# Two-layer expert kernel after windowed attention: routing in groups of 4, 2, 2, 2, 2 and visits of two tiles at the end

## The chip, the core and the metric

The kernel runs on one core of one Trainium2 chip. The metric is device time in microseconds (us) of one execution; the number given is the median of three. Beside it stands one execution taken with the hardware profiler, from which all rows below come.

## What is computed

```python
def reference(q, k, v, n_global, n_local, ...):
    # 2 batches, 8 heads, 768 tokens, head size 64; 8 global keys, a window of 96
    attn_out = _attn_ref(q, k, v, n_global, n_local)      # softmax over the window and the global keys, ALiBi bias
    x = attn_out.transpose(0, 2, 1, 3).reshape(1536, 512)
    x = _moe_ref(x, ...)          # RMS norm; (silu(xn @ w_gate) * (xn @ w_val)) @ w_out, d_ff 1536
    return _moe2_ref(x, ...)      # noisy top-2 routing over 8 experts, then relu(x @ w1[e]) @ w2[e], d_ff 1024

def _moe2_ref(x, w_gate, w_noise, noise, w1, w2):
    noisy_logits = x @ w_gate + np.log1p(np.exp(x @ w_noise)) * noise
    top2 = np.argpartition(-noisy_logits, 2, axis=1)[:, :2]
    top2_w = softmax of the two chosen logits
    for e in range(8):
        for k in range(2):
            mask = top2[:, k] == e
            h = np.maximum(x[mask] @ w1[e], 0.0)
            out[mask] += top2_w[mask, k, None] * (h @ w2[e])
```

The weights of the first layer and the inputs are 64-bit floats that the kernel converts word by word (`conv`). Products are made in a split form: each operand is a rounded high part (h) and a remainder (l), and TensorE multiplies h by h, h by l and l by h.

## The kernel before

The 1536 tokens are 12 tiles of 128. Three stages run one after the other and overlap at their borders.

**Attention.** 12 tiles of 4 units (pairs of heads) each. `scores`, `turn` and `values` of a unit are spread over three slots; `norm` transposes the finished tile into `xTh`/`xTl`. The first 12 slots run alone, the others are worked in between the steps of the first layer (`side`). In the same time `feed` calls `conv`, which converts one block of the first layer's weights: ScalarE takes the absolute value (L517), VectorE clips, shifts and merges words (L518 to L525; the clip goes to GpSimd for blocks f of 2 and more), and a block of `g`, `v` and `o` is three conversions. Blocks with f of 2 and more are ordered behind tile 1's norm (`after`), those with f of 0 and 1 are not.

**First layer.** The 12 blocks of d_ff lie in four chunks (`CHUNKS`: 0 to 2, 3 to 5, 6 and 7, 8 to 11). `VISITS` is the list of (chunk, first tile, number of tiles). A step is one f of one visit: `up` makes 12 matmuls for the gate and 12 for the value (L572), `hidden` makes the tanh (L580), two VectorE products (L581, L582), the split dh (L585) and dl (L586), and `finish`, one step later, calls `down` (L599). A step of two tiles has both products in one bank of PSUM (`pz`, 256 columns each), one of four tiles in two (`pg`, `pv`, 512 columns each). Attention's scratch memory (pool `at`) is closed when attention is written out, and pool `late`, called "b" in the code, takes its place; `hidden` takes its u, dh and dl from "b" once that is there. After the last chunk a tile is complete: it is stored to `x2d` in HBM on SyncE's queue (L612), and when the tiles of a routing group are complete, `route` is called.

**Routing.** `GS` is the list of group sizes in tiles. For a group, `route` transposes its tiles (L649), computes the router's logits (L653), two activations (L661, L662), the top 2, the prefix sums that give each token its slot (L680 to L683), and writes token number and weight to the table `metad` by one indirect DMA of GpSimd for each tile and choice (L729, "scatters"): two for each tile. After group `LEAD` the expert with the most tokens so far is chosen (`lead`), and SyncE reads its number (L916).

**Second layer.** `units[0]` and `units[1]` both work that expert: unit 0 its first 256 slots, from the groups up to `LEAD`, and unit 1 the other 256. Seven more units, one for each other expert, follow in the order that the last group's counts give (`order`, L745, read by SyncE at L967). A unit fetches its slots (`me`, L768), clips them (`ic`, L777), gathers the rows of `x2d` with indirect DMAs (`xg`, L786), transposes them (`pg`, L796; L798, L799) and runs `up` (L822) and `down` (L844 or L838) on weights that SyncE loads (`wab`, L752 and L755) and ScalarE, VectorE and GpSimd split (`sa`, `sb`: L556, L558). Unit 1's slots are fetched after group `LEAD + 1`; the last group, which comes later than that fetch, is added to them on the chip (`late_slots`: `idf` L624, `hot` L629, matmuls L634, then `ic`). Each unit adds its result to `out` by a gather (L804) and a scatter (L876).

A scheduler at build time sets the order of instructions on each engine from the program text and its own estimate of durations; so an edit in one place can move instructions elsewhere. Each engine runs its own list in order and waits at an instruction whose inputs are not there; a DMA that SyncE, ScalarE or GpSimd issues is such an instruction of its list. Buffers of one tag rotate: a new tile waits until the last reader of the old one is done.

Of the kernel before, what the change touches and what calls it, by code (L numbers as in the profile page):

```python
# [9 lines left out]
F32 = mybir.dt.float32  # L10
# [9 lines left out]
P = 128  # L20
# [85 lines left out]
def fused(ctx: ExitStack, tc: tile.TileContext, q, k, v, n_global, n_local, w_gate, w_val, w_out,  # L106
# [12 lines left out]
    FB2 = F2 // P  # L119
    GS = [4, 4, 2, 2]  # L120
    NG = len(GS)
    G0 = [sum(GS[:g]) for g in range(NG)]
    LEAD = 1
    ST = 4
    CHUNKS = [[0, 1, 2], [3, 4, 5], [6, 7], [8, 9, 10, 11]]
    VISITS = [(0, 2 * i, 2) for i in range(6)] + [(1, 4 * i, 4) for i in range(3)]
    VISITS += [(c, t, 4) for c in (2, 3) for t in (0, 4)] + [(2, 8, 4), (3, 8, 2), (3, 10, 2)]
    FEED = [0, 0, 1, 0, 2, 2, 2, 2, 2, 3, 3]
    START = 12
    LAG = 8  # L130
    NRAW = {"a": 12, "b": 8}
    NACC = 8
# [375 lines left out]
    def conv(nm, f, src):  # L508
# [11 lines left out]
        sh = nc.vector.tensor_scalar(wi, wi, 3, 0x3FFFFFF8, op0=ALU.logical_shift_left, op1=ALU.bitwise_and)  # L520
        if late:
            after(ab, "A", 1)
            after(sh, "V", 1)
        nc.vector.scalar_tensor_tensor(wi, hi, -0x40000000, wi, op0=ALU.bitwise_and, op1=ALU.bitwise_or)
# [50 lines left out]
    def hidden(ci, f, t0, nt, pg, pv):  # L575
        GN = nt * P
        hp = pools.get("b", at)
        wd = 512 if "b" in pools else 256
        u = hp.tile([P, wd], F32, name=f"u{t0}_{f}", tag="u", bufs=1)[:, :GN]
        nc.scalar.activation(u, pg, AF.Tanh, scale=0.5)  # L580
        nc.vector.scalar_tensor_tensor(u, u, 1.0, pg, op0=ALU.add, op1=ALU.mult)  # L581
        nc.vector.scalar_tensor_tensor(u, u, 0.5, pv, op0=ALU.mult, op1=ALU.mult)  # L582
        dh = hp.tile([P, wd], F32R, name=f"dh{t0}_{f}", tag="dh", bufs=2)
        dl = hp.tile([P, wd], F32R, name=f"dl{t0}_{f}", tag="dl", bufs=2)
        nc.scalar.activation(dh[:, :GN], u, AF.Copy)  # L585
        (nc.gpsimd if ci < len(CHUNKS) - 1 else nc.vector).tensor_sub(dl[:, :GN], u, dh[:, :GN].bitcast(F32))  # L586
        return dh, dl

    def down(ci, t0, nt, f, d):
# [12 lines left out]
        for t in range(nt):  # L602
# [7 lines left out]
            if ci == len(CHUNKS) - 1:  # L610
                x2t[ti] = accs[ti]
                nc.sync.dma_start(x2d[ti * P:(ti + 1) * P, :], accs[ti])  # L612
        if t0 + nt == NT // P:
# [26 lines left out]
    def route(g):  # L640
# [3 lines left out]
        for t in range(GT):  # L644
            ti = G0[g] + t
            pt = ps.tile([P, 512], F32, name=f"pr{ti}", tag="ts"[t % 2 if last else 0])
            p3 = pt.rearrange("p (a b) -> p a b", a=DC)
# [241 lines left out]
    while n < START:  # L889
        slot(n, 0)  # L890
        slot(n, 1)
        if n in (3, 6, 9):
            feed(3)
        n += 1
    prev = None
    todo = []
# [13 lines left out]
    def finish(ci, t0, nt, f, d):  # L910
        down(ci, t0, nt, f, d)
        if ci == len(CHUNKS) - 1 and f == CHUNKS[ci][-1] and t0 != G0[-1]:
            g = G0.index(t0)
            route(g)
            if g == LEAD:
                r = nc.sync.value_load(lead.bitcast(I32)[:1, :1], min_val=0, max_val=E - 1)  # L916
                units[0].e = units[1].e = r
            if g == LEAD + 1:
                units[1].fetch()

    for vi, (ci, t0, nt) in enumerate(VISITS):
# [9 lines left out]
        for f in CHUNKS[ci]:  # L931
# [19 lines left out]
            prev = (ci, t0, nt, f, d)  # L951
            if (ci, t0) == (2, 8):
                if f == CHUNKS[ci][1]:
                    units[0].slots()
                    units[0].gather(0)
                    units[0].gather(1)
            if ci == 3 and t0 >= 8:
                k = CHUNKS[ci].index(f) + (4 if t0 == 10 else 0)
                if k in (2, 3):
                    units[0].turn(k - 2)  # L960
                moe2_weights(0, units[0].e, k)
    finish(*prev)
# [116 lines left out]
```

## Time and profile before

| what | value |
| --- | --- |
| three executions | 867.02, 864.85, 859.6 us; median 864.85 |
| profiled execution | 865.25 us; span 863.5 us (first to last instruction) |
| mean granted TensorE clock | 0.947 of full speed |
| busy share: TensorE, its weight loads, VectorE, ScalarE, GpSimd | 92%, 81%, 55%, 41%, 36% |
| span by stage, from the timeline | attention to about 220 us, first layer's last matmul at 498, second layer to the end |

The profiled execution is within 0.1% of the median, so sums made on its rows stand against both. What lies outside the span is 865.25 - 863.5 = 1.75 us.

How the rows are read: a row of a timeline is start, duration, engine, line, operation, output from input, shape, and in brackets the idle time of the engine just before it and what ended it. A row of waits is the waiting instruction, what it waited for, total, times and longest. A row of stretches is the stretch, its length, the busy time (and instructions) of PE, PEld, DVE, ACT and POOL, the granted clock as a share of full speed, the share of the DMA engines and GB/s. A row of groups is line, operation, shapes and count, then busy time, mean ns of one, and idle time before. PE is TensorE, PEld its weight loads, DVE VectorE, ACT ScalarE, POOL GpSimd, SP SyncE.

### The profile page before, as it was taken

The numbers are of one execution on the slowest core, as the hardware profiler recorded it, in microseconds if no ns is written. First come the engines' busy times: TensorE is split into PE (matmuls) and PEld (weight loads), VectorE is DVE, ScalarE is ACT, GpSimd is POOL, SyncE is SP. The second block draws the span as 40 slices with busy tenths as digits, with TensorE's granted clock in tenths as the row PEclk, the third lists the DMA queues.
The fourth block names the chain that finished last, engine by engine and source line by source line (L and its number), as shares of the span: only waits on it lengthen the run. The fifth ranks groups of instructions, "written<-read, shape, count | busy, mean of one in ns | idle before, by whom it ended". The sixth has DMA issues, their size and how long they took to land. (4 is left out here: it accounts for less than half of the span.)

```text
span 863.5 us, 13789 instructions
## 1 busy us (share of the span) xinstructions
PE 798.6 (92%) x5040; PEld 698.0 (81%) x5040; DVE 473.5 (55%) x1036; ACT 356.1 (41%) x780; POOL 314.3 (36%) x348
## 2 busy tenths in 40 slices
PE   5799899999699999999999685999999999999993
PEld 4568688898688888888889575878899999999982
DVE  5857966666678886323345342754444444545541
ACT  5556656655453333111323251543334343443440
POOL 7526434231565553100042333333252524334321
PEclk9759999999799999999999885999999999999997
DMA  9424422160133330001010504379063738282710
GB/s 193 130 62 135 132 52 63 38 184 14 50 121 100 98 98 25 1 0 49 1 50 10 162 26 121 91 226 277 1 204 116 235 105 252 68 270 70 252 47 33
DMA packets 117126, 89.81 MB, mean 104 GB/s; under 512 B 49481, under 2 KB 100681, under 8 KB 117056
## 3 DMA queue, kind: packets, MB, share of 16 engines
q1 hardware_dynamic: 106864, 68.24, 28.0%
q0 software_dynamic: 7440, 20.32, 6.9%
q8 instruction: 41, 0.67, 0.3%
q10 hardware_dynamic: 2752, 0.34, 0.3%
q14 instruction: 29, 0.24, 0.1%
HBM read 76.23 MB, written 13.34 MB: 104 GB/s over the span
## 5 line engine op out<-in xcount | busy, mean ns | idle before, releaser
L822 PE MATMUL pz<-gh,sa 128*128 128x256 f32 (+7 forms) x576 | 160.0, 344 | 9.7 <-ACT sa L556 9.7
L822 PEld LDWEIGHTS pz<-gh,sa 128*128 128x128 f32 x576 | 106.1, 192 | 15.0 <-ACT sa L556 9.9
L822 PE MATMUL pz<-gl,sa 128*128 128x256 f32 (+7 forms) x288 | 98.4, 342 | 0.0
L599 PE MATMUL acc<-wo,dh 128*128 128x512 f32 x288 | 87.8, 402 | 5.1 <-ACT dh L585 5.1
L838 PE MATMUL ac<-zh,sb 128*128 128x480 f32 (+4 forms) x320 | 85.8, 361 | 0.0
L826 ACT ACTIVATE zh<-pz 128x256 fp32r<-128x256 f32 (+7 forms) x72 | 35.2, 488 | 108.9 <-PE pz L822 108.0
L586 POOL TENSOR_TENSOR dl<-u,dh 128x256 fp32r<-128x256 f32 (+1 forms) x33 | 34.4, 1042 | 123.9 <-ACT dh L585 113.9
L827 DVE SCALAR_TENSOR_TENSOR zl<-pz,zh 128x256 fp32r<-128x256 f32 (+7 forms) x72 | 39.7, 552 | 69.3 <-ACT zh L826 69.1
L556 ACT ACTIVATE sa<-wab 128x512 fp32r<-128x512 f32 x72 | 45.3, 630 | 74.7 <-PE ac L838 35.8
L558 POOL TENSOR_TENSOR sa<-wab,sa 128x512 fp32r<-128x512 f32 x21 | 27.1, 1289 | 116.6 <-ACT sa L556 115.7
L599 PEld LDWEIGHTS acc<-wo,dh 128*128 128x128 f32 x288 | 52.8, 190 | 16.5 <-ACT dh L585 5.7
L572 PE MATMUL pg<-xTh,wg 128*128 128x512 f32 x184 | 61.8, 396 | 0.0
L572 PE MATMUL pv<-xTh,wv 128*128 128x512 f32 x184 | 61.7, 396 | 0.0
L838 PEld LDWEIGHTS ac<-zh,sb 128*128 128x128 f32 x320 | 59.0, 188 | 3.0
L558 DVE TENSOR_TENSOR sa<-wab,sa 128x512 fp32r<-128x512 f32 x51 | 35.5, 695 | 45.3 <-ACT sa L556 44.0
L358 PE MATMUL ps<-kT,qT 64*128 64x256 f32 (+1 forms) x248 | 55.8, 372 | 4.6 <-DVE mx L362 3.9
L822 PEld LDWEIGHTS pz<-gl,sa 128*128 128x128 f32 x288 | 55.2, 192 | 2.7
L599 PE MATMUL acc<-wo,dl 128*128 128x512 f32 x144 | 54.2, 411 | 1.4 <-POOL dl L586 1.4
L365 ACT ACTIVATE p<-s,mx 128x256 f32<-128x256 f32 (+1 forms) x96 | 46.2, 483 | 22.6 <-DVE mx L362 22.5
L838 PE MATMUL ac<-zl,sb 128*128 128x480 f32 (+4 forms) x160 | 52.7, 358 | 0.0
L876 POOL DMA_INDIRECT out_dram<-y,me x30 | 31.2, 1040 | 56.5 <-DVE y L875 51.9
L844 PE MATMUL ac<-sb,zh 128*128 128x512 f32 (+1 forms) x160 | 51.6, 408 | 0.0
(223 smaller groups left out, 1934.0 us busy)
## 6 DMA issues: line engine op xcount, KB each, us to landing
wab<-in_moe_w_dram SPq DMA_DIRECT2D x128, 256.0 KB, 7.3
rg<-in_moe_w_gate_dram SPq DMA_DIRECT2D x12, 512.0 KB, 3.5
rv<-in_moe_w_val_dram SPq DMA_DIRECT2D x12, 512.0 KB, 3.5
ro<-in_moe_w_out_dram SPq DMA_DIRECT2D x12, 512.0 KB, 3.6
kn<-in_k_dram SPq DMA_DIRECT2D x12, 256.0 KB, 3.3
qn<-in_q_dram SPq DMA_DIRECT2D x12, 256.0 KB, 4.3
vn<-in_v_dram SPq DMA_DIRECT2D x12, 256.0 KB, 4.3
out_dram<-zero SPq DMA_DIRECT2D x1, 3072.0 KB, 13.5
```

The lines of the kernel that those rows point to most:

```text
L358: nc.tensor.matmul(o, qT[a][sl, h // 2, :], kT[c][sl, h // 2, C0:], start=(n == 0), stop=(n == len(prods) - 1))
L365: nc.scalar.activation(p[:, :W], s[:, :W], AF.Exp, scale=-1.0, bias=mx[:, h:h + 1], accum_out=sm[:, h:h + 1])
L556: nc.scalar.activation(wp[:, 0], src, AF.Copy)
L558: (nc.gpsimd if pool else nc.vector).tensor_sub(wp[:, 1], src, wp[:, 0].bitcast(F32))
L572: nc.tensor.matmul(pz, a[:, cs], x[:, tt:tt + nt, c, :], start=(n == 0), stop=(n == 3 * DC - 1))
L586: (nc.gpsimd if ci < len(CHUNKS) - 1 else nc.vector).tensor_sub(dl[:, :GN], u, dh[:, :GN].bitcast(F32))
L599: nc.tensor.matmul(acc[t], a[:, tt], w, start=(f == CHUNKS[ci][0] and n == 0), stop=(end and n == 2))
L822: nc.tensor.matmul(pz[:, :cap], a[:, cs], x[:, c, :cap], start=(k == 0), stop=(k == 3 * DC - 1))
L826: nc.scalar.activation(dh[:, :cap], pz[:, :cap], AF.Relu)
L827: nc.vector.scalar_tensor_tensor(dl[:, :cap], pz[:, :cap], 0.0, dh[:, :cap].bitcast(F32), op0=ALU.max, op1=ALU.subtract)
L838: nc.tensor.matmul(acc[c][:, :cap], w[:, c * P:(c + 1) * P], a[:, :cap], start=(f == 0 and k == 0), stop=(f == FB2 - 1 and k == 2))
L844: nc.tensor.matmul(acc[s][:m], a[:, ss], w, start=(f == 0 and k == 0), stop=(f == FB2 - 1 and k == 2))
```

## The change

Five things, all in the function `fused`:

1. `GS` becomes 4, 2, 2, 2, 2 and `LEAD` 2: unit 0 still takes the tokens of the first eight tiles, but the group that completes them has two tiles. The visits (3, 4, 4) and (2, 8, 4) become pairs of two-tile visits.
2. The weights of unit 0: the first two of eight blocks are loaded right after the lead expert's number is read, and each later block is called for two steps earlier in the list (`FEEDS`). Slots and gathers of unit 0 are called at the step (2, 10, 6), its transposes at the second and third step of (3, 8).
3. The stores of `x2d` are issued by ScalarE.
4. `hidden` takes its three tiles for two-tile visits from pool `sb`, in a size of their own, at all times; pool "b" has seven buffers of the tag `raw` and not eight.
5. The conversion of the block f = 1 is ordered behind tile 0's norm. The transposes of `route` rotate over three banks.

```diff
-    GS = [4, 4, 2, 2]
+    GS = [4, 2, 2, 2, 2]
...
-    LEAD = 1
+    LEAD = 2
...
-    VISITS += [(c, t, 4) for c in (2, 3) for t in (0, 4)] + [(2, 8, 4), (3, 8, 2), (3, 10, 2)]
+    VISITS += [(2, 0, 4), (2, 4, 4), (3, 0, 4)] + [(c, t, 2) for c, t in ((3, 4), (3, 6), (2, 8), (2, 10), (3, 8), (3, 10))]
...
-    NRAW = {"a": 12, "b": 8}
+    NRAW = {"a": 12, "b": 7}
...
-        if late:
-            after(ab, "A", 1)
-            after(sh, "V", 1)
+        if f:
+            after(ab, "A", min(f, 2) - 1)
+            after(sh, "V", min(f, 2) - 1)
...
-        hp = pools.get("b", at)
-        wd = 512 if "b" in pools else 256
-        u = hp.tile([P, wd], F32, name=f"u{t0}_{f}", tag="u", bufs=1)[:, :GN]
+        hp = pools["b"] if nt > 2 else sb
+        u = hp.tile([P, GN], F32, name=f"u{t0}_{f}", tag="u", bufs=1)
...
-                nc.sync.dma_start(x2d[ti * P:(ti + 1) * P, :], accs[ti])
+                nc.scalar.dma_start(x2d[ti * P:(ti + 1) * P, :], accs[ti])
...
-            pt = ps.tile([P, 512], F32, name=f"pr{ti}", tag="ts"[t % 2 if last else 0])
+            pt = ps.tile([P, 512], F32, name=f"pr{ti}", tag=("t", "t2", "s")[t % 3])
...
+    FEEDS = {x: k for k, x in enumerate([(2, 10, 6), (2, 10, 7)] + [(3, 8, f) for f in CHUNKS[3]])}
...
                 units[0].e = units[1].e = r
+                for f2 in range(2):
+                    moe2_weights(0, r, f2)
...
-            if (ci, t0) == (2, 8):
-                if f == CHUNKS[ci][1]:
-                    units[0].slots()
-                    units[0].gather(0)
-                    units[0].gather(1)
-            if ci == 3 and t0 >= 8:
-                k = CHUNKS[ci].index(f) + (4 if t0 == 10 else 0)
-                if k in (2, 3):
-                    units[0].turn(k - 2)
-                moe2_weights(0, units[0].e, k)
+            kx = FEEDS.get((ci, t0, f))
+            if kx == 0:
+                units[0].slots()
+                units[0].gather(0)
+                units[0].gather(1)
+            if kx in (3, 4):
+                units[0].turn(kx - 3)
+            if kx is not None and kx < FB2 - 2:
+                moe2_weights(0, units[0].e, kx + 2)
```

Lines from 576 on stand one lower in the changed kernel up to line 890 (L768 becomes L767).

**SyncE, from the lead expert's number to the first weights.** A row is line, operation and transfer; `ISA` rows are address arithmetic. Before:

```order
L916 TENSOR_LOAD lead
L916 ISA x2
L612 DMA x2d<-x_8_3600 128x512
L612 DMA x2d<-x_9_3602 128x512
L768 ISA
L768 DMA me_5260<-metad 128x2x2
L752 ISA
L752 DMA wab_0_5319<-in_moe_w_dram 128x4x128
L755 ISA
L755 DMA wab_0_5319<-in_moe_w_dram 128x512
```

After:

```order
L916 TENSOR_LOAD lead
L916 ISA x2
L751 ISA
L751 DMA wab_0_5366<-in_moe_w_dram 128x4x128
L754 ISA
L754 DMA wab_0_5366<-in_moe_w_dram 128x512
L751 ISA
L751 DMA wab_1_5369<-in_moe_w_dram 128x4x128
L754 ISA
L754 DMA wab_1_5369<-in_moe_w_dram 128x512
L767 ISA
L767 DMA me_5454<-metad 128x2x2
```

The stores have left this queue, and two blocks of weights stand ahead of the fetch of unit 0's slots; the other six blocks follow it without a break, and the second fetch (unit 1's) stands behind the last of them, where before it stood between block 3 and block 4.

**GpSimd, the scatters into the slot table.** `si_*` are the slots of one group. Before:

```order
L729 DMA metad<-meta,si_4831 4096x2 x8
L586 TENSOR_TENSOR dl_7_5241<-u_7_5236,dh_7_5240 128x512
L729 DMA metad<-meta,si_5167 4096x2 x8
L786 DMA xg_0_5266<-x2d,ic_5262 128x512
L786 DMA xg_1_5268<-x2d,ic_5262 128x512
```

After:

```order
L728 DMA metad<-meta,si_4830 4096x2 x8
L728 DMA metad<-meta,si_5082 4096x2 x4
L585 TENSOR_TENSOR dl_6_5253<-u_6_5248,dh_6_5252 128x256
L585 TENSOR_TENSOR dl_7_5402<-u_7_5397,dh_7_5401 128x256
L585 TENSOR_TENSOR dl_6_5443<-u_6_5438,dh_6_5442 128x256
L585 TENSOR_TENSOR dl_7_5497<-u_7_5492,dh_7_5496 128x256
L728 DMA metad<-meta,si_5335 4096x2 x4
L558 TENSOR_TENSOR sb_0_0_6176<-wab_0_5366,sb_0_0_6176 128x512
L785 DMA xg_0_5460<-x2d,ic_5456 128x512
L785 DMA xg_1_5462<-x2d,ic_5456 128x512
```

The scatters ahead of unit 0's gathers are 8, 4 and 4 where they were 8 and 8, and the last four stand behind the remainders of the visits (2, 8) and (2, 10).

**VectorE, tile 1's first unit.** `pl` are the remainders that attention's value product waits for, `wcg` and `wcv` the words of the block f = 1, `x` the finished tile 0. Before:

```order
L382 SCALAR_TENSOR_TENSOR pl_3_344<-pp_3_340,ph_3_343 128x2x128
L518 TENSOR_SCALAR wcg_484<-wcg_484 128x512
L520 TENSOR_SCALAR wcg_484<-wcg_484 128x512
L524 SCALAR_TENSOR_TENSOR wcg_484<-rg_482,wcg_484 128x512
L525 SCALAR_TENSOR_TENSOR wcg_484<-rg_482,wcg_484 128x512
L518 TENSOR_SCALAR wcv_495<-wcv_495 128x512
L520 TENSOR_SCALAR wcv_495<-wcv_495 128x512
L382 SCALAR_TENSOR_TENSOR pl_0_376<-pp_0_370,ph_0_375 128x512
L524 SCALAR_TENSOR_TENSOR wcv_495<-rv_493,wcv_495 128x512
L525 SCALAR_TENSOR_TENSOR wcv_495<-rv_493,wcv_495 128x512
L420 TENSOR_TENSOR x_419<-po_259,rs_416 128x512
```

After:

```order
L382 SCALAR_TENSOR_TENSOR pl_3_344<-pp_3_340,ph_3_343 128x2x128
L382 SCALAR_TENSOR_TENSOR pl_0_376<-pp_0_370,ph_0_375 128x512
L420 TENSOR_TENSOR x_419<-po_259,rs_416 128x512
L362 ISA s_4_444,mx_347<-nbias,ps_2_441 128x256
L362 ISA mx_347 128x1
L362 ISA s_6_448,mx_347<-nbias,ps_2_441 128x256
L362 ISA mx_347 128x1
```

Eight conversions of f = 1 that stood ahead of tile 0's x now stand behind it, among the units of tiles 1 and 2.

## Rows read from the trace of the kernel before

**Rows 1.** What TensorE waited for over the whole span: microseconds in total, times, longest.
```profile
PE pz L822 <- ACT sa L556: 9.7, 2, 8.9
...
PE acc L599 <- ACT dh L585: 5.1, 2, 4.6
...
PE pg L796 <- DMA xg<-x2d,ic: 4.5, 2, 2.4
```

**Rows 2.** Busy time of the engines and TensorE's granted clock by stretch, 490 to 538.
```profile
490.00:498.00 8.00, 5.57 (x19) 4.07 (x18) 4.88 (x6) 2.33 (x5) 3.62 (x3) 0.50 0.70 246
498.00:518.00 20.00, 16.30 (x119) 14.59 (x117) 9.88 (x47) 11.90 (x22) 6.47 (x6) 0.93 0.08 28
518.00:526.00 8.00, 0.30 (x5) 0.21 (x5) 1.77 (x17) 0.00 (x0) 0.54 (x2) 0.50 0.17 43
526.00:538.00 12.00, 10.64 (x43) 10.04 (x44) 3.56 (x11) 3.18 (x6) 8.01 (x8) 0.50 0.56 154
```

**Rows 3.** Timeline of SyncE's queue: start, duration, line, transfer.
```profile
484.16 0.41 SPq L768 DMA_DIRECT2D me<-metad  x1
...
522.93 0.40 SPq L768 DMA_DIRECT2D me<-metad  x1
```

**Rows 4.** Timeline of GpSimd: the last scatter of the third group.
```profile
517.07 0.99 POOL L729 DMA_INDIRECT metad<-meta,si  x1 [0.30 <-issue]
```

**Rows 5.** Timeline of VectorE: start, duration, line, operation, idle time before and its releaser.
```profile
467.91 0.17 DVE L713 CAST si<-sl 128x8 int32<-128x8 f32 x1
...
486.39 0.17 DVE L777 TENSOR_SCALAR ic<-me 128x2 int32<-128x2 int32 x1 [8.60 <-DMA me<-metad]
...
512.73 0.17 DVE L713 CAST si<-sl 128x4 int32<-128x4 f32 x1 [0.21 <-DVE sl L711]
...
524.75 0.17 DVE L624 CAST idf<-me 128x2 f32<-128x2 int32 x1 [5.19 <-DMA me<-metad]
```

**Rows 6.** Timeline of TensorE: last up, gathered rows, unit 0's wait, unit 1's first matmul.
```profile
483.69 0.28 PE L572 MATMUL pz<-xTh,wv 128*128 128x256 f32 x1
...
493.40 1.08 PE L796 MATMUL pg<-ident,xg 128*128 128x128 f32 x4 [2.44 <-DMA xg<-x2d,ic]
...
527.36 0.58 PE L822 MATMUL pz<-gh,sa 128*128 128x256 f32 x1 [8.93 <-ACT sa L556]
...
548.91 0.28 PE L822 MATMUL pz<-gh,sa 128*128 128x256 f32 x1
```

**Rows 7.** Timeline of ScalarE: tanh of two-tile steps that follow each other.
```profile
471.44 0.39 ACT L580 ACTIVATE u<-pz 128x256 f32<-128x256 f32 x1 [2.58 <-PE pz L572]
...
475.56 0.39 ACT L580 ACTIVATE u<-pz 128x256 f32<-128x256 f32 x1 [2.24 <-PE pz L572]
```

**Rows 8.** TensorE's groups from 385 to 484, two routed groups of four tiles: matmuls of route.
```profile
L653 PE MATMUL lg<-wr,x2T 128*128 128x16 f32 x64 | 7.7, 252 | 0.0
L649 PE MATMUL pr<-ident,x 128*128 128x128 f32 x32 | 5.0, 279 | 0.0
```

**Rows 9.** Timeline of ScalarE at attention's end.
```profile
222.00 0.36 ACT L580 ACTIVATE u<-pz 128x256 f32<-128x256 f32 x1
```

**Rows 10.** Timeline of TensorE there.
```profile
223.55 0.58 PE L572 MATMUL pz<-xTh,wg 128*128 128x256 f32 x1 [2.69 <-DVE u L582]
```

**Rows 11.** One stretch there: busy time and clock.
```profile
222.00:226.00 4.00, 2.45 (x11) 2.45 (x12) 1.66 (x4) 2.63 (x7) 3.92 (x5) 0.50 0.02 6
```

**Rows 12.** Timeline of VectorE near the start: f = 1, first and last of twelve.
```profile
29.25 0.78 DVE L518 TENSOR_SCALAR wcg<-wcg 128x512 f32<-128x512 f32 x1 [1.11 <-ACT wcg L517]
...
41.45 0.68 DVE L525 SCALAR_TENSOR_TENSOR wco<-ro,wco 128x512 int32<-128x512 int32 x1
```

**Rows 13.** Two stretches near the start: busy time and clock.
```profile
32.00:38.00 6.00, 2.19 (x40) 1.79 (x37) 5.46 (x14) 3.78 (x9) 2.63 (x3) 1.00 0.89 223
38.00:46.00 8.00, 8.00 (x41) 5.25 (x40) 6.30 (x20) 5.32 (x18) 2.27 (x3) 0.54 0.30 95
```

**Rows 14.** Line 612, the stores of x2d: durations in ns, first and last start.
```profile
L612 SPq DMA_DIRECT2D x2d<-x x12: 319/320/347, 395.8 to 498.8; - x12
```

More of the change, by code (lines that the diff above doesn't have):

```diff
@@ L582, in hidden @@
         nc.vector.scalar_tensor_tensor(u, u, 0.5, pv, op0=ALU.mult, op1=ALU.mult)
[L583 to L586, printed above, removed]
+        dh = hp.tile([P, GN], F32R, name=f"dh{t0}_{f}", tag="dh", bufs=2)
+        dl = hp.tile([P, GN], F32R, name=f"dl{t0}_{f}", tag="dl", bufs=2)
+        nc.scalar.activation(dh, u, AF.Copy)
+        (nc.gpsimd if ci < len(CHUNKS) - 1 else nc.vector).tensor_sub(dl, u, dh.bitcast(F32))
         return dh, dl
```

## Prediction

> **What bounds the kernel now.** I read the waits of TensorE first, since it is busy in 92% of the span: nothing but its own idle time and its clock can give much. The longest wait is 8.9 us of unit 0 for split weights, the next 4.6 us for a dh of the first layer; gathered rows cost 4.5 us in two waits [rows 1]. All of these lie between 484 and 538 us, the border of the two layers. The stretches show the rest of the damage there: TensorE is idle 2.43, 3.70, 7.70 and 1.36 us in the four of them (length less busy time), and in three the granted clock is 0.50 of full speed, 1.2 GHz of 2.4, each time during or after an idle stretch [rows 2]. Its 5.57 us and 10.64 us of work at half speed would be 2.8 and 5.3 us at full speed. With the 4.6 us just before [rows 1] the place is worth 4.6 + 2.4 + 3.7 + 7.7 + 1.4 + 2.8 + 5.3 = 28 us; that is all that a better border can give.
>
> Why it waits is in SyncE's queue. The fetches of the slots are issued at 484.16 and 522.93 [rows 3]. The last scatter that the second one needs was issued at 517.07 [rows 4]; the fetch comes 5.86 us after it, because it waits until the scatters have landed. Everything behind a fetch in that in-order queue waits too, the weights among it; so does VectorE at ic (8.60 us) and at idf (5.19 us) [rows 5], and behind ic stand products of the first layer, which is why TensorE waits for dh. After the first layer's last up matmul (483.69 + 0.28 = 483.97) unit 1's first matmul comes only at 548.91 [rows 6].
>
> **Groups and early weights.** The amount of matmul work is the same: four-tile steps become twice as many two-tile steps with the same columns; I count nothing for it, within 1 us. Two-tile steps follow each other at 475.56 - 471.44 = 4.12 us [rows 7]; with the spread of the neighbours I use 4.2. Routing costs TensorE (7.7 + 5.0) / 8 = 1.6 us a tile [rows 8]. Before the first layer's last up now ten tiles are routed, not eight, and unit 0's two transposes lie there (4 matmuls each like route's, 0.63 us): 483.97 + 2 x 1.6 + 1.3 = 488.5.
>
> First fetch. In the order, si of the third group stands on VectorE just ahead of the products of step (3, 8, 8), which ends seven steps earlier, with 4.5 us of routing and transposes in between: 488.5 - 29.4 - 4.5 = 454.6, against 467.91 for the si that the first fetch needed in before [rows 5]. In before the third group's four scatters took 517.07 - 512.73 = 4.3 us from its si to the last issue [rows 4, 5], so here the last is at 458.9, the fetch 5.86 us later at 464.8, and ic another 2.2 us later (486.39 - 484.16 [rows 3, 5]), 467.0. In VectorE's list ic stands ahead of the products of (3, 8, 10), which could start at about 463. So VectorE still stalls some 4 us, but TensorE has the next step's up in the other bank; it loses between 0 and 3 us, and I take 1.5, as the next up covers most of it. The gathered rows were there 493.40 - 486.39 = 7.0 us after ic [rows 5, 6], so here at 474, before TensorE wants them in (3, 10, 9), which starts at about 475. The weights have come before the fetch. So of the first stall's 4.6 + 4.5 us and the slow clock after it, 1.5 us stays. The first layer's last up then ends at 490.
>
> Second fetch. The fourth group's si stands behind the first layer's last remainder on VectorE, about 495. As in before, idf follows si by 524.75 - 512.73 = 12.0 us [rows 5]: 507. All weights of unit 0 have been loaded by then. TensorE has, from 490 on, two downs, the last two tiles to route and unit 0's first two or three blocks of up and down: by the length of a step (4.2, of which a down is about a third) and of routing I estimate 3 + 3 + 9 = 15 us, until 505. So idf still makes a stall, about 3.5 us counting what ScalarE and VectorE need after it, where before it was 7.7; bounds 0 (if more of unit 0's splits are ready) and 7.7 (if nothing of it was gained). From idf to unit 1's first matmul before took 548.91 - 524.75 = 24.2 us, some 5 us of it lost to half clock [rows 2]; after a shorter stall I expect 20 to 24, so unit 1 starts at 527 to 531, I take 530. **That is 19 us earlier than 548.91**, bounds 10 and 25. From there on both kernels run the same units.
>
> The fetch's landing time is where a rule speaks against my row. The 5.86 us above is from the last scatter's issue to the fetch. The Trainium skill, "DMA: Bandwidth & Descriptors", section "Anatomy of one DMA — SWDGE (gpsimd) path", puts the fixed cost of such a DMA at about 2.0 us. By it the fetch would come about 3 us after the issue, the second stall would vanish, and the sum would be some 3 us lower; the trace does not agree, so the row stays.
>
> **Buffers.** One raw buffer less (7) makes block 1's weights wait for the last use of a converted block of chunk 2, and blocks 2 to 7 likewise; in the built order those uses end with step (3, 10, 8), before unit 0 needs the blocks. Cost 0, covered by the first layer's last four steps; if that cover is gone, a wait of pz for sa comes back, up to the 8.9 us of [rows 1].
>
> **End of attention.** In before, the u of the first two-tile step that runs after attention lies in memory that attention frees only at its end: its tanh comes at 222.00 [rows 9], TensorE idles 2.69 us before 223.55 [rows 10], and runs at half clock after it, 2.45 us of work [rows 11]. With tiles of their own these steps can start earlier and fill the gaps of the last units. But the order now puts the last tile's norm and transposes right behind attention's last product, a chain of about 5 us with little beside it. The place holds 2.69 + 1.2 and some smaller gaps; bounds +6 and -2, I take 3.
>
> **Start.** The twelve conversions of f = 1 occupy VectorE from 29.25 to 41.45 [rows 12], ahead of what attention's first tiles wait for; TensorE is busy 2.19 of 6 us there, and at clock 0.54 in the next 8 us [rows 13]. They are moved behind tile 0's x, where they are in the way of tiles 1 and 2 instead, some 8 us of VectorE in all. In 38 to 46 TensorE has no idle time and the clock is low all the same, so one gap less need not raise it: the gap is worth up to 3.8 us, the clock up to 4 more; the other end is -4, if the conversions only make the next gap. I take 3.
>
> **Stores.** Twelve issues of 0.32 us leave SyncE [rows 14], which waited rather than worked, and come to ScalarE, 41% busy: 0. Each pair waits there for VectorE's adds with a tanh behind it; ScalarE sits idle 2.58 and 2.24 us before a tanh [rows 7], so a hold shorter than that costs nothing. Rotating route's banks: 0, at most 0.3 us gained. One more group adds a chain of two activations and their table loads on ScalarE, off TensorE's path while steps remain: 0.
>
> **Sum.** 865.25 - 19 - 3 - 3 = 840.25, so 840 us. The profiled time is 0.4 us above the median, which changes nothing.
>
> **Rivals.** (a) The late chain keeps its length: the second scatters, fetch, idf, hot and gathers follow each other whatever stands before them, and unit 1 starts at about 539 with half clock kept. For it speaks that SyncE's second fetch now stands behind all weights and that si waits for the last remainder; against it that the second group's si has four steps less ahead. 865 - 10 - 1 = 854. (b) Start and end of attention give more, because the clock comes back at full speed some 8 us earlier: 831. Against it speaks the low clock with no idle time in 38 to 46 [rows 13]. (c) The change doesn't do what it says: the first fetch stalls VectorE as long as before, since its landing sets it, and new gaps eat the rest: 862. (d) Slower: the stores on ScalarE hold the tanhs. If VectorE's adds come more than about 2.4 us after ScalarE reaches a store, the hold goes to TensorE. Six pairs at 2 us, each followed by half clock like the 2.8 us lost in 490 to 498 [rows 2], is 29 us: 840 + 29 = 869. It decides from the point where VectorE stalls at ic or idf while a store's add stands behind; both stalls are forecast shorter, which speaks against it, as does the idle time before the tanhs.
>
> **How the numbers follow.** Forecast 840 (832 to 848): 0.52. (a) 854: 0.20. (b) 831: 0.13. (c) 862: 0.08. (d) 869: 0.07. A change of about 1%, 8.6 us, is what a measurement of this kernel can tell from none. Faster by more than that, below 856: the forecast, (b), and most of (a), 0.82; within it 0.11; slower 0.07. The range leaves out (c) and (d) and a little of (b): 828 to 856.
>
> **What will show it.** Right: SyncE's first fetch before 470 with two blocks of weights ahead; no wait of TensorE for dh above 2 us; the wait of pz for sa below 5 us; unit 1's first matmul at 527 to 531 after taking off what start and attention gave; more granted clock between 490 and 540. Wrong: idf as late as 515, a TensorE wait behind tanh that ends with a store on ScalarE, unit 1's slots still arriving after unit 0 has run out, or a new gap where attention's last tile is normed. The number falls most easily if start or attention's end moves by more than its 3 us, since the order of instructions there is new in many places that the rows of before can't price.

## The result, and the profile after

| | before | after |
| --- | --- | --- |
| median (lowest to highest, 4 runs each) | 862.5 (859.6 to 867.02) us | 849.82 (847.18 to 853.01) us |
| profiled execution, span | 865.25, 863.5 us | 851.79, 850.1 us |
| mean granted clock | 0.947 | 0.960 |

The ratio is 0.985, 95% interval 0.981 to 0.988: faster by 1.5%. The forecast was 840 us, with 828 to 856 as the range.

To see where the 13.4 us of the two spans come from, I cut both at the same events: the first xTh of tile 8 (attention two thirds done), two tanhs of the first layer's middle (the 25th and the 35th of all; 299.38 and 383.17 in before, 298.16 and 381.04 after), the last transposes of unit 2's gathered rows, and the last matmul. The 14.4 us behind the last matmul are alike in all kernels.

| stretch (us) | before | after | difference |
| --- | --- | --- | --- |
| start, to tile 8's xTh | 183.7 | 180.2 | -3.5 |
| attention's end, to the first tanh | 115.7 | 118.0 | +2.3 |
| middle, to the second tanh | 83.8 | 82.9 | -0.9 |
| border, to unit 2's last transposes | 190.6 | 176.4 | -14.1 |
| rest of the second layer | 275.4 | 278.2 | +2.8 |

**The border.** TensorE is idle 21.9 us of this stretch in before and 11.4 us in after, which is 10.5 of the 14.1 us; its busy time falls by the other 3.6 us, with a mean granted clock of 0.97 where before had 0.91. Its waits after, over the whole span (total, times, longest):

```profile
...
PE px L483 <- DVE x L470: 5.0, 1, 5.0
PE pg L795 <- DMA xg<-x2d,ic: 3.6, 1, 3.6
...
PE pz L821 <- ACT sa L556: 2.5, 4, 0.8
PE pz L821 <- DVE sa L558: 2.5, 2, 2.3
PE acc L598 <- ACT dh L584: 2.4, 1, 2.4
```

Against [rows 1], the 8.9 us for split weights are down to 2.3, the 4.6 us for dh to 2.4; the 5.0 us for x (VectorE) is not at the border. The stretches of after answer to [rows 2]:

```profile
463.00:470.00 7.00, 4.55 (x22) 3.77 (x21) 3.64 (x6) 2.62 (x6) 2.08 (x2) 0.76 0.81 246
...
484.00:500.00 16.00, 16.00 (x122) 15.05 (x121) 7.62 (x36) 6.47 (x13) 3.38 (x4) 1.00 0.06 17
...
508.00:520.00 12.00, 9.74 (x72) 8.81 (x72) 10.19 (x44) 5.66 (x11) 6.17 (x6) 1.00 0.03 2
520.00:528.00 8.00, 4.39 (x26) 3.58 (x26) 4.25 (x16) 2.96 (x6) 2.48 (x3) 0.92 0.52 66
528.00:538.00 10.00, 10.00 (x53) 9.17 (x52) 5.88 (x11) 4.26 (x8) 2.27 (x3) 0.72 0.14 52
```

Where before had 0.50 in three stretches, after has 1.00 but for three of those shown: 0.76 and 0.92, with idle time of 2.45 and 3.61 us in them, and 0.72 right behind the second. SyncE's fetches and VectorE's late chain, against [rows 3, 5], and GpSimd's last scatters ahead of each fetch and of unit 1's gathers [rows 4]:

```profile
465.04 0.37 SPq L767 DMA_DIRECT2D me<-metad  x1
...
506.55 0.37 SPq L767 DMA_DIRECT2D me<-metad  x1
```

```profile
508.35 0.17 DVE L623 CAST idf<-me 128x2 f32<-128x2 int32 x1 [4.58 <-DMA me<-metad]
...
515.05 0.17 DVE L712 CAST si<-sl 128x4 int32<-128x4 f32 x1
...
518.90 0.34 DVE L776 TENSOR_SCALAR ic<-me 128x2 int32<-128x2 int32 x1
```

```profile
457.96 0.97 POOL L728 DMA_INDIRECT metad<-meta,si  x1 [0.30 <-issue]
...
499.87 0.97 POOL L728 DMA_INDIRECT metad<-meta,si  x1 [0.31 <-issue]
...
519.55 0.97 POOL L728 DMA_INDIRECT metad<-meta,si  x1 [0.30 <-issue]
520.83 0.99 POOL L785 DMA_INDIRECT xg<-x2d,ic  x1 [0.30 <-issue]
```

The fetches come 19.1 and 16.4 us earlier. They stand 465.04 - 457.96 = 7.08 and 506.55 - 499.87 = 6.68 us behind the last scatter that they need; in before it was 6.83 us for the first fetch and 5.86 for the second. Unit 1's rows are gathered at 520.83, behind the last group's four scatters in GpSimd's list, although its ic was there at 519.2. TensorE gets them at 527.70 (against [rows 6]):

```profile
476.65 0.60 PE L795 MATMUL pg<-ident,xg 128*128 128x128 f32 x4
...
510.66 0.51 PE L821 MATMUL pz<-gh,sa 128*128 128x256 f32 x2 [2.26 <-DVE sa L558]
...
527.70 1.09 PE L795 MATMUL pg<-ident,xg 128*128 128x128 f32 x4 [3.61 <-DMA xg<-x2d,ic]
...
532.00 0.63 PE L821 MATMUL pz<-gh,sa 128*128 128x256 f32 x2
```

The last group's slots (si) have another place beside idf than in before, where they came 0.21 us after it (against [rows 5]):

```profile
524.96 0.17 DVE L713 CAST si<-sl 128x4 int32<-128x4 f32 x1
```

There VectorE had worked that group's routing before it waited at idf (its last step but the cast to si starts at 519.38). In after this routing stands behind idf, and si comes 515.05 - 508.35 = 6.70 us later. So the way from idf to unit 1 holds more work than the row of before that the prediction took for it.

**The first stall.** The prediction put it on VectorE, at ic. ScalarE's list of after reads otherwise:

```profile
459.92 0.39 ACT L579 ACTIVATE u<-pz 128x256 f32<-128x256 f32 x1 [3.66 <-PE pz L572]
464.70 0.63 ACT L556 ACTIVATE sa<-wab 128x512 fp32r<-128x512 f32 x1 [4.40 <-DMA wab<-in_moe_w_dram]
465.24 0.40 ACT L584 ACTIVATE dh<-u 128x256 fp32r<-128x256 f32 x1
```

VectorE's last product of that u starts at 460.80 and takes 0.42, so dh could have begun at about 461.3. It begins at 465.24: the split of unit 0's first weights stands ahead of it on ScalarE and waits for them to land (issued at 458.36 and 459.11). Before had the same pair, seen in ScalarE's timeline there:

```profile
487.58 0.63 ACT L556 ACTIVATE sa<-wab 128x512 fp32r<-128x512 f32 x1 [7.38 <-DMA wab<-in_moe_w_dram]
488.12 0.40 ACT L585 ACTIVATE dh<-u 128x256 fp32r<-128x256 f32 x1
```

There VectorE's products came behind ic as well, and both causes ended within 1 us of each other; so [rows 5] alone could not tell them apart.

**Attention's end.** The first two-tile step that was held in before [rows 9] has its tanh at 204.75, 17 us earlier. But after the last attention product there is now nothing left to work (against [rows 10]):

```profile
227.34 0.87 PE L483 MATMUL px<-ident,x 128*128 128x128 f32 x3 [4.99 <-DVE x L470]
```

**Start.** Four stretches of after, then the last two of them in before (the first two are near [rows 13]):

```profile
30.00:40.00 10.00, 10.00 (x98) 8.79 (x100) 7.68 (x28) 7.60 (x21) 1.60 (x3) 0.74 0.24 55
40.00:48.00 8.00, 4.79 (x82) 3.93 (x79) 8.00 (x17) 6.45 (x18) 3.90 (x4) 1.00 0.57 157
...
85.00:100.00 15.00, 13.39 (x83) 11.23 (x84) 11.84 (x32) 8.97 (x25) 7.73 (x7) 0.55 0.37 96
...
125.00:140.00 15.00, 14.66 (x96) 13.33 (x97) 6.50 (x24) 5.95 (x23) 6.62 (x9) 0.66 0.23 45
```

```profile
85.00:100.00 15.00, 13.30 (x122) 9.72 (x121) 14.96 (x33) 10.82 (x28) 10.10 (x10) 1.00 0.47 124
...
125.00:140.00 15.00, 14.52 (x149) 11.90 (x148) 7.88 (x29) 9.08 (x29) 6.90 (x10) 1.00 0.33 71
```

Tile 2's xTh comes at 71.69, 10.1 us earlier than 81.77. Of that 3.5 us are left at tile 8: the clock is at 0.55 and 0.66 in two later stretches in which before had full speed.

### The profile page after: what moved, and what is told of

Its sections match the earlier page's. It is cut to its first block, busy times and chain, and to the rows that moved or that the text cites. A ratio compares the mean times of both kernels' runs of the same rounds, so it can differ in the third digit from the quotient of the medians.

```text
span 850.1 us, 14111 instructions
## 1 busy us (share of the span) xinstructions
PE 796.6 (94%) x5180; PEld 701.0 (82%) x5180; DVE 474.0 (56%) x1069; ACT 358.3 (42%) x797; POOL 314.9 (37%) x350
## 5 line engine op out<-in xcount | busy, mean ns | idle before, releaser
L821 PEld LDWEIGHTS pz<-gh,sa 128*128 128x128 f32 x576 | 104.4, 189 | 13.4 <-DVE sa L558 4.2
L572 PE MATMUL pz<-xTh,wg 128*128 128x256 f32 x304 | 67.5, 299 | 1.0 <-ACT xTh L488 0.7
L572 PE MATMUL pz<-xTh,wv 128*128 128x256 f32 x304 | 62.4, 286 | 0.0
L728 POOL DMA_INDIRECT metad<-meta,si x24 | 24.2, 1010 | 97.7 <-DVE si L712 90.8
L572 PEld LDWEIGHTS pz<-xTh,wg 128*128 128x128 f32 x304 | 53.1, 202 | 4.3 <-ACT xTh L488 1.1
```

Of the source, the lines that this page charges most:

```text
L572: nc.tensor.matmul(pz, a[:, cs], x[:, tt:tt + nt, c, :], start=(n == 0), stop=(n == 3 * DC - 1))
L728: st = nc.gpsimd.indirect_dma_start(out=metad, out_offset=bass.IndirectOffsetOnAxis(ap=si[:, t, kk:kk + 1], axis=0), in_=meta[:, G0[g] + t ...
L821: nc.tensor.matmul(pz[:, :cap], a[:, cs], x[:, c, :cap], start=(k == 0), stop=(k == 3 * DC - 1))
```

## The experiments

Each undoes or changes one thing in the changed kernel (e11: in the kernel before); e8 to e10 and e12 build on the run that they name. "Border" and the other stretches are those of the table above. Before ran beside them at 862 to 865 us.

**e1_conv_old: the conversions of f = 1 back where they were.**

```diff
-        if f:
-            after(ab, "A", min(f, 2) - 1)
-            after(sh, "V", min(f, 2) - 1)
+        if late:
+            after(ab, "A", 1)
+            after(sh, "V", 1)
```

> The changed kernel, with the conversions of f = 1 free of tile 0's norm again, as in before. In the changed kernel's trace the transposes of tiles 0 to 2 come 8 to 11 us earlier than in before, those of tiles 6 to 8 only 3 to 4 us. Theory A, the conversions' order made the 10 us and new slow-clock stretches at 85 to 100 and 127 to 137 took 7 of them back: tiles 0 to 2 go back by about 10 us, tile 8 by 3, and the time is about 853. Rival B, the whole of it is lost again by attention's end whatever the start: tile 8 as in the changed kernel, time within 1.5 us of its 849.8. Rival C, the late losses have another cause and the start is worth its 10 us: about 860.

857.45 us; ratio 0.994 (0.991 to 0.996). The start is 185.1 us, 4.9 more than after, the border 176.3, as after. So the start's edit is worth some 5 us by the stretch and 7.6 by the medians, more than forecast. Tile 2's xTh is back at 82.78, and the stretches of 85 to 100 and 125 to 140 are both at 1.00 again, with TensorE busy 12.88 and 14.52 us: the same edit wins the first 10 us and brings the slow stretches. From tile 2 to tile 8 TensorE is busy 98.3 us in before and 105.6 in after, with mean clocks of 0.98 and 0.89, and idle 3.7 and 2.9 us; what is lost there is lost in slower work.

**e2_hidden_old: u, dh and dl of a step from attention's memory again, as in before.**

```diff
-        hp = pools["b"] if nt > 2 else sb
+        hp = pools.get("b", at)
+        wd = 512 if "b" in pools else 256
...
```

> The changed kernel, with the old tiles of hidden: u, dh and dl of two-tile visits from attention's pool until it is closed and from the late pool after that. Theory A, tiles of their own only pull work ahead of attention's end that is missing there, so that the chain of the last tile's norm stands bare (5.0 us): the steps of (0, 8) go back to about 220 us, the 5.0 us wait of px for x shrinks below 3, and the time is within 2 us of 849.8. Rival B, the prediction's: slower by 3, about 853. Rival C, the bare chain and the slow clock behind it cost more than the earlier steps gave: faster by 3 to 5, about 846.

847.31 us; ratio 0.981 (0.976 to 0.985). Attention's end takes 111.9 us, 6.0 less than after: the 4.99 us wait for x is replaced by the old one of 2.69 us behind u. The border is 3.6 us longer, so that 2.5 us are left in the medians, where the two intervals overlap.

**e3_stores_sync: the stores of x2d on SyncE's queue.**

```diff
-                nc.scalar.dma_start(x2d[ti * P:(ti + 1) * P, :], accs[ti])
+                nc.sync.dma_start(x2d[ti * P:(ti + 1) * P, :], accs[ti])
```

> The changed kernel, with the stores of x2d issued by SyncE again. Theory A, the stores' place is worth nothing either way: within 2 us of the changed kernel's 849.8, same waits at the border. Rival B, on SyncE each pair that waits for VectorE's adds holds the weights and the fetch behind it: slower by 3 to 5, with later fetches. Rival C, on ScalarE they hold splits and tanhs (one store there takes 2.67 us at 498.6 with ScalarE idle 4.08 us): faster by 2 to 3.

854.7 us; ratio 0.990 (0.986 to 0.994). The border is 181.7 us, 5.3 more. All three of its waits grow in the trace:

```profile
PE pg L795 <- DMA xg<-x2d,ic: 4.8, 2, 2.8
PE acc L598 <- ACT dh L584: 3.8, 1, 3.8
PE pz L821 <- DVE sa L558: 3.4, 1, 3.4
```

The intervals of this kernel and after just touch; medians and border agree on some 5 us. So the stores were not free where they were. The early weights are split later here though they are issued as early (457.81; sa at 465.56 against 464.70). Counted from the second tanh, the fetches come only 0.3 and 0.4 us later, so rival B's late fetches are not what costs; half of the 5.3 us is there at unit 1's transposes, the rest comes until unit 2's. By which path the stores' place does that I have not isolated.

**e4_weights_late: no weights ahead of the first fetch.** The two `moe2_weights` calls at `LEAD` are dropped; all eight blocks are loaded in the steps of (3, 8) and (3, 10).

> The changed kernel, with all weights of unit 0 called in the last eight steps of the first layer, as in before, so none ahead of the fetch. Theory A, with the lead group closed some 13 us earlier the fetch no longer holds anything up, so the weights' place is worth 0 to 3 us: waits of pz for sa stay below 3 us, time 850 to 853. Rival B, the early weights carry the border's gain: waits of pz for sa of 8 us or more come back, and the time is about 860.

855.22 us; ratio 0.989 (0.983 to 0.994). The border is 181.3, 4.9 more; the wait for dh goes, and the one for gathered rows is 7.5 us in two. By the stretch the early weights are worth 5 us, in spite of the wait of 2.4 us that they bring; the intervals of this kernel and after overlap, so the times alone don't show it. The kind of stall that the prediction described is to be seen here: with no weights ahead, VectorE waits 3.67 us at ic, ahead of a dl, and TensorE 1.21 us for that dl.

**e5_groups_old: groups of 4, 4, 2, 2 and the old visits.**

```diff
-    GS = [4, 2, 2, 2, 2]
+    GS = [4, 4, 2, 2]
-    LEAD = 2
+    LEAD = 1
...
```

> The changed kernel, with the old groups 4, 4, 2, 2, the old visits and LEAD 1; early weights, stores and all the rest as changed. Theory A, the groups make most of the border's 14 us, because scatters, landing and fetch of the lead group start 13 us earlier: the fetch of unit 0 goes back to about 480, TensorE waits for dh again by 3 to 5 us and for rows by 4, and the time is about 859. Rival B, the weights ahead of the fetch were what mattered: the border loses at most 4 us, time about 853.

857.36 us; ratio 0.993 (0.990 to 0.996). The border is 182.0 (+5.6), the wait for gathered rows 7.1 us in three. The fetch of unit 0 is at 480.41, TensorE's wait for dh 1.8 us. By the medians the groups are worth 7.5 us, as much as the start's edit; 2.5 of them lie in the rest of the second layer (280.6), for which no cause is shown.

**e6_hold_last_step: one step of the first layer is kept for attention's end.** The first up matmul of step (0, 8, 2) is ordered behind attention's last po matmul.

> The changed kernel, with one order more: the first up matmul of step (0, 8, 2) stays behind attention's last value product. Nothing else is undone, hidden keeps its own tiles. Theory A, what costs at attention's end is only the lack of cover for the last norm's chain: the wait of px for x (5.0 us) goes below 2, the stretch from tile 8's xTh to step (1, 8, 5)'s tanh shrinks from 118 to about 112 us as it did with the old tiles, the border stays at 176, time about 844. Rival B, the old tiles' gain there came from their slower attention steps and not from the cover: the stretch stays at 116 or more, time about 848.

848.06 us; ratio 0.982 (0.976 to 0.988). The wait of px is gone; in its place stands one of 1.90 us:

```profile
224.10 1.20 PE L601 MATMUL acc<-wo,dh 128*128 128x512 f32 x4 [1.90 <-ACT dh L587]
```

Attention's end takes 110.6 us, 7.4 less, with a clock of 1.00 from 215 to 235, where after has 0.83. (The stretch ends at the 25th tanh, which is step (1, 8, 3), not (1, 8, 5).) So the wait and its slow clock are what the own tiles cost. The border did not stay: it is 179.2, 2.7 more, and of the gain 1.8 us are left in the medians, where the intervals overlap.

**e7_idf_behind_hot: idf, which waits for the second fetch, behind the four hot tiles on VectorE.**

> The changed kernel, with idf ordered behind the hot tiles on VectorE, so that VectorE does not wait for the second fetch ahead of the last group's routing and of unit 0's splits. Theory A, that wait (4.6 us of VectorE, 2.3 of TensorE) is on the path: TensorE's wait of pz for sa at 508 goes, the last group's slots come 1 to 2 us earlier, the border shrinks by 2 to 4 us, time about 847. Rival B, unit 1's start hangs on the landing of its rows alone: the 3.6 us wait before its transposes grows by what the other loses, time as the changed kernel's within 1 us.

851.99 us; ratio 0.987 (0.983 to 0.990). TensorE's 2.26 us for sa fall to 0.85, but the wait before unit 1's transposes grows from 3.61 to 5.6:

```profile
PE pg L796 <- DMA xg<-x2d,ic: 7.0, 2, 5.6
```

The border stays, 176.9, and counted from the second tanh the last group's si comes as late as in after (134.1 and 134.0 us). The second stall is therefore not VectorE's at idf; what ends last is the chain of the last group: its logits, slots, hot, ic, gathers.

**e8_hidden_old_raw8: e2 with eight raw buffers.**

```diff
-    NRAW = {"a": 12, "b": 7}
+    NRAW = {"a": 12, "b": 8}
```

> The changed kernel with the old tiles of hidden, as in the earlier run, and with eight raw buffers. From unit 2's last transpose to the last matmul before took 275.4 us, the changed kernel 278.2, and the four kernels with seven buffers that ran since 277.2 to 280.6. Theory A, the missing buffer costs that, by weights that land late in units 3 and 4: this stretch goes back to 275.5 and the time is 2 to 3 below the 847.3 of the same kernel with seven. Rival B, the stretch depends on when the weights' loads meet the gathers: it stays at 277 or more, and the time at 847.

852.92 us; ratio 0.987 (0.983 to 0.991). The rest of the second layer takes 278.6 us with eight buffers too. The missing buffer does not explain the +2.8 of after. The median is 5.6 us above that of e2, which neither theory said; the border is 181.5.

**e9_ic_behind: e6, and ic out of the way.** The first fetch is called where it was; ic and the gathers are called at step (3, 8, 10), ic ordered behind that step's second product, and the transposes three steps later, at (3, 10, 8) and (3, 10, 9).

```diff
...
+            if n == 0:
+                follow(clip.ins, state["u"])
...
```

> The kernel of the run with the held step (0, 8, 2), and unit 0's ic ordered behind the products of step (3, 8, 10), its transposes called two steps later. Theory A, the wait of the first layer's down for dh at 457 to 461 us (2.4 to 3.8 us in all kernels with two-tile groups) is VectorE standing at ic ahead of those products: it goes, TensorE runs through until the first layer's end, and the border's first part (97 us in the held kernel) shrinks by about 3 us; the time is 845. Rival B, the chain of the last group, from the first layer's last sums to unit 1's rows, starts earlier by the same but waits elsewhere, so that the wait before unit 1's transposes (4.0 us) does not change: still 3 faster. Rival C, the rows of unit 0 then come too late and the wait moves to its transposes: time as the held kernel's 848.

848.03 us; ratio 0.982 (0.978 to 0.987), as e6; border 179.4. TensorE's wait for dh stays, at 4.2 us, with ic behind the products. My theory of the first stall fell here, and ScalarE's timeline of this kernel shows the other:

```profile
460.18 0.63 ACT L557 ACTIVATE sa<-wab 128x512 fp32r<-128x512 f32 x1 [6.16 <-DMA wab<-in_moe_w_dram]
460.72 0.40 ACT L587 ACTIVATE dh<-u 128x256 fp32r<-128x256 f32 x1
```

**e10_scatters_behind: e9, and the last group's scatters behind unit 1's gathers on GpSimd.** The loop of scatters is called after `nxt.gather` and ordered behind the last gather.

> The same, and the last group's four scatters on GpSimd ordered behind the two gathers of unit 1. Theory A, the gathers wait for GpSimd, which works at four scatters of 1.3 us when ic is ready (gather issued 1.6 us after ic in the changed kernel): the gathers go 1 to 2 us earlier, the wait before unit 1's transposes shrinks by as much, and unit 2's fetch, which waits for the scatters, still comes in time; 1 to 2 us faster than the kernel before it. Rival B, the scatters then delay unit 2's fetch and its rows: the wait before unit 2's transposes grows by more than that.

846.36 us; ratio 0.980 (0.976 to 0.985). GpSimd's list is now

```profile
516.51 0.96 POOL L797 DMA_INDIRECT xg<-x2d,ic  x1 [0.30 <-issue]
517.77 1.00 POOL L732 DMA_INDIRECT metad<-meta,si  x1 [0.30 <-issue]
```

and no wait for gathered rows is left among TensorE's longer ones; 2.9 us for a split sb and 2.3 for unit 1's gh came up in their place. The border is 178.5, 0.9 less than in e9; the medians, 1.7 us apart, don't separate the two.

**e11_before_raw7: the kernel before with seven raw buffers.**

> The kernel before, with seven raw buffers in pool b, nothing else. From unit 2's last transpose to the last matmul before took 275.4 us, all kernels with the change's other parts 277 to 281, the one with eight buffers too (278.6). Theory A, the buffer count is one of two things that can cost it: this kernel shows 277 or more there, and its time is 2 to 3 above the kernel before. Rival B, seven buffers cost nothing there: 275.4, time as before within 1.5 us; the loss then comes from when the loads of a unit meet the gathers.

867.04 us against 864.8; ratio 1.003 (1.000 to 1.006). The rest of the second layer is 277.3, 2.0 more; the border is 1.8 less, so the profiled execution is as long as that of before.

**e12_splits_behind: e10, and the splits of unit 0's weights on ScalarE behind the first layer's dh** (that of step (3, 8, 11)).

```diff
-        nc.scalar.activation(wp[:, 0], src, AF.Copy)
+        copy = nc.scalar.activation(wp[:, 0], src, AF.Copy)
+        if u == 0:
+            follow(copy.ins, state["dh"])
...
```

> The kernel of e10, and in it the splits of unit 0's first weights on ScalarE are ordered behind the hidden product dh of the first MoE's last step (3, 8, 11). Theory A (the first stall at the border is ScalarE's: a split that waits for the early weights stands ahead of dh): TensorE's wait of acc for dh, 4.0 us in e10, falls to under 1 us, the border goes from 178.5 to some 175 us, and the time to some 843 us beside 846.4 in e10. Rival B (the split is needed as early as that): the wait moves to unit 0's first up product, pz for sa, or to its first pg, and the time stays within 1 us of e10's.

837.86 us; ratio 0.969 (0.965 to 0.974), an interval that lies below that of after and of e10. ScalarE's order is now

```profile
463.69 0.38 ACT L584 ACTIVATE u<-pz 128x256 f32<-128x256 f32 x1 [4.92 <-DVE dl L592]
465.01 0.42 ACT L589 ACTIVATE dh<-u 128x256 fp32r<-128x256 f32 x1 [0.94 <-DVE u L586]
465.34 1.14 ACT L557 ACTIVATE sa<-wab 128x512 fp32r<-128x512 f32 x2
```

dh again follows its product after the usual 0.94 us, and the 4.0 us that TensorE waited at 456.39 in e10 are gone; 1.25 us for a dl are left. That dl stands behind ic on VectorE, which waits 4.78 us for the fetched slots: the kind of stall that the prediction described, now without the other. The border is 171.1, 7.4 less than in e10 and 19.4 less than before; the rest of the second layer is 275.4, the length of before, with seven buffers. Attention's end took back 1.9. The time came out 5 us below what my theory forecast: the border is 3.9 us shorter than forecast and the second layer 2.4. Neither was foreseen. TensorE is idle 13.4 us of the border in e10 and 7.4 here, so more than the first stall went; of the waits behind it, the one for gathered rows is 1.0 us, that for sa 2.5.

## Why the prediction was right, and where it was not

The forecast was 840, the time 849.8: the sign is right and the border is where the gain lies, but only about half of the forecast gain came (12.7 of some 25 us in medians). Of the prediction's signs, the fetch before 470, the wait for sa below 5 us and the better clock came true; the wait for dh is 2.45 us, not below 2, and the gap at attention's last tile, named as a sign of being wrong, is there. By steps:

- **Groups and early weights, 19 us: measured 14.1.** What the forecast said of the fetches holds: first fetch 465 (465.04), ic 467.0 (467.66), last scatter 458.9 (457.96), idf 507 (508.35). e5 and e4 show that both edits count, 5.6 and 4.9 us of border. Unit 1's first matmul is at 532.00; the kernel reaches the border 2.1 us earlier (381.04 against 383.17), so 534.1 compares with the forecast 530, and 14.8 us with the 19. What was mis-sized:
  - *The first stall, 1.5 us: 2.45 us, and a clock of 0.76 in the stretch that holds it.* The cause given was wrong. It was VectorE's list that I read for what stands ahead of a product, and not ScalarE's, where a split that waits for weights stands ahead of dh. That the weights come before the fetch is true (split at 464.70, fetch at 465.04), but ScalarE had stood idle for them since 460.31. e9 took ic away and the wait stayed; e12 took the split away and the wait for dh went. The price put on ic itself holds where the split is out of the way: 1.21 us in e4 and 1.25 in e12 against the 1.5. The early weights, which shorten unit 0, brought this wait forward with them.
  - *idf to unit 1.* The row of before had the last group's routing behind it already, and after has not (6.70 us from idf to si against 0.21). Here rival (a), the late chain, was right in part: the chain from idf through hot, ic, four scatters and the gathers to unit 1's first matmul took 532.00 - 508.35 = 23.7 us, at the upper end of the 20 to 24. e7 shows that the chain and not idf ends last, e10 that scatters ahead of the gathers hold them.
- **The landing of scatters.** The row's 5.86 us was used, the shorter of the two in before; here it is 7.08 and 6.68. The Trainium skill, "DMA: Bandwidth & Descriptors", section "Anatomy of one DMA — SWDGE (gpsimd) path", gives about 2.0 us as the fixed cost. These traces still don't agree, so following the row was right.
- **Attention's end, -3 us: measured +2.3**, just outside the bounds. The chain of about 5 us with little beside it was named, and not counted against the gain. The gap is there at 4.99 us, since steps with tiles of their own are worked ahead and none is left to cover it (e6). Undoing only the tiles (e2) gives -3.8 against before.
- **Start, -3 us: measured -3.5**, and 4.9 by e1. Right in size, but not by the steps given: 10.1 us were won at tile 2, and 6.6 of them lost until tile 8, in stretches of low clock that before did not have there and that the same edit brings (e1).
- **Buffers, 0: the rest of the second layer is 2.8 us longer.** TensorE waits for sa at two changes of units there, 673.30 to 674.07 and 714.40 to 715.05; it is idle 1.6 of the 2.8 us in all, and not at all in this stretch of before. In before the stretch is 2.0 us longer with seven buffers (e11); but e8 has eight and the delay stays, e12 seven and has none. So neither the count alone nor any other cause is shown; it may be when the weights' issues fall beside the unit's end, which was not tried alone.
- **Stores, 0: worth 5 us** (e3), on the side of the gain. Rival (d), that they hold tanhs on ScalarE, did not happen, nor did (c): the first fetch came as early as forecast. That SyncE "waited rather than worked" was no ground for pricing them at nothing; by which path they cost time on SyncE is open. This gain that the sum did not hold is luck: with the stores on SyncE the time is 854.7, 1.3 us from the end of the range.

The terms that fell on the wrong side, attention's end by 5.3 us, the border by 4.9 and the second layer by 2.8, make 13.0; start and middle gave back 0.5 and 0.9. The 11.6 us left are, within rounding, what lies between the sum's 840.25 and the profiled 851.79.

## What to carry to other kernels

When TensorE waits for an operand, read the list of every engine on the operand's path, and ask of each what stands just ahead and what that waits for: a copy of freshly loaded weights, queued ahead of a running layer's activation, stops both. A load that is issued earlier wants its first consumer placed later, or the early load brings its wait along. Work that is freed to run sooner no longer covers the gap that it used to cover; so look, for each step that a change pulls ahead, at what it stood beside.

## What the hardware showed that I had not expected

- From the issue of the last indirect scatter to the dependent fetch it took 6.83 and 5.86 us in before, 7.08 and 6.68 after; in the last of these SyncE issued nothing in between. For units 0 and 1 it is 5.02 (unit 0 in e4, with no weights ahead of the fetch) to 9.27 us (unit 0 in e5) over all runs.
- Full clock gained at the start did not last: 0.55 and 0.66 from 85 to 100 and 125 to 140, with TensorE busy 13.39 and 14.66 of 15 us, where before had 1.00 with 13.30 and 14.52 busy, and so had e1, with 12.88 and 14.52. What set the clock there is open.
